# Products of zeros on an idle TensorE, GpSimd's sums in smaller pieces, and three placings moved, in an attention and expert kernel

## The chip, the cores and the metric

The kernel runs on one core of a Trainium2 chip. A core has five engines that run side by side, each through its own instructions in program order: TensorE (PE, matrix products and transposes), VectorE (DVE), ScalarE (ACT), GpSimd (POOL) and SyncE (SP), which here issues nearly all transfers. The metric is the device time of one execution in microseconds; the median over several runs is compared.

## The reference, cut to what matters

Attention over blocks, then a top-one mixture of experts, then a dense layer with a mish-like activation, each feeding the next:

```
k_sum = k.reshape(B, H, nb, 32, D).max(axis=3)        # 24 blocks of keys: maxima
v_sum = v.reshape(B, H, nb, 32, D).mean(axis=3)       # and of values: means
scores = [q k^T / 8 where |i - j| < 16, q k_sum^T / 8 + log 32]
a      = softmax(scores);  x = a [v, v_sum]           # B=2, H=8, S=768, D=64
logits = x w_gate + modality_bias[modality_id]        # 1536 tokens, 8 experts
out[e == argmax] = gate * (relu(x w1[e]) w2[e])       # 512 -> 1024 -> 512
h = out w_in;  y = (h * tanh(softplus(h))) w_out      # 512 -> 2048 -> 512
```

## The kernel before

The program has three stages that follow each other: attention with the gate (to about 130 us), the experts, the dense layer. The change touches the first alone. It is written by hand in the order in which each engine is to run: there is no scheduler, and an instruction waits only for what it reads or overwrites.

Attention goes through 24 groups (`groups`), each of 128 query positions of one batch and half of the heads (`hh`, four heads): six groups of batch 0 with half 0, six with half 1, then twelve of batch 1 with the halves in turn. The loop over `g` is a pipeline that runs two groups ahead: iteration g makes the scores of group g + 2, transposes the weights of group g (`transpose_a`, `store_aT`) and multiplies those of group g - 1 with the values (`values`, `store_xT`). Per group: `scores` (a bf16 product that lays the mask into PSUM, then q k in f32; both for four tiles), `top` (VectorE's row maximum `nm`), `exps` (ScalarE, with the row sum `sm`), `sums` (VectorE: a 128x4 addition and a reciprocal), `normalize` (`an`, on VectorE or GpSimd by the string `norm_by`). From group 10 on `gate_products` follows, which reads the tables `gm`; `choose` reads the table `bias_t`.

Queries and keys come in chunks of 256 positions (`c` = 0 to 2). A chunk (b, hh, c) is loaded by SyncE, packed by one engine (`pack`, tile `hp`), transposed on TensorE and copied from PSUM: `k_chunk` into `kt`, `q_chunk` in two halves of 64 partitions into one of four block-diagonal buffers `qb`. The table `prep` says in which iteration a chunk is taken up, who packs it and who copies: ("q", 1, 0, 0, "G", "VV") is packed by GpSimd, both halves copied by VectorE. Packs of `prep[g + 1]` stand at the start of iteration g, the transposes of `prep[g]` after its scores. "kw" entries make the block maxima (`k_maxima`), the overlapping windows of keys (`k_windows`, tile `kw`) and spread the maxima (`k_blocks`); they run one iteration after the one they are listed under.

The means of the values are made on GpSimd from a tile `vb` of 96 partitions (four heads of 24 blocks) x 32 positions x 64: `v_means` adds halves together, 16 + 16 positions (level 1, 1024 elements a partition), then 8 + 8, 4 + 4, 2 + 2, 1 + 1 and a scaling (level 2). Entries "m1" and "m2" of `prep` place the levels; there are four such sums, one for each batch and half, two of which run through both levels at once. The result is written to `vw` by four transfers (`store_means`), listed in `means_at`.

Ahead of the loop stand the loads of the first chunks, the first transposes, the scores of groups 0 and 1, and `small_loads` with `gate_tables` (the gate's identity columns, the modality's mask `mf`, its products `mt` and their sum `bias_t`, nine instructions on GpSimd). SyncE issues the loads in one order: those of the table `loads` for iteration g + 1 are issued at the start of iteration g, as far as buffers and the transfer queue let it run ahead.

## Time and profile before

| | before |
|---|---|
| median of three runs | 571.78 us (569.55 to 576.25) |
| profiled execution, device time | 573.32 us |
| its span, first to last instruction | 571.3 us |
| TensorE products busy | 533.4 us, 93% |
| VectorE busy | 390.7 us, 68% |
| ScalarE busy | 387.2 us, 68% |
| GpSimd busy | 95.5 us, 17% |

The page counts busy time over the whole span. Rows of the timeline give the start in us, the length in us, engine, line of the kernel, operation, tile written <- tiles read, shapes and a count of instructions merged into the row; in brackets the idle time of the engine ahead of it and what ended that. "PEclk" is the share of full speed that TensorE's clock was granted: 1.00 is 2.4 GHz, 0.5 is 1.2 GHz. The record of the clock begins at its first change; the first 23 us read 1.00 for that reason alone.

### The profile page before, as it was taken

How to read it: one execution, taken by the hardware profiler on the slowest of the kernel's cores; microseconds unless marked ns; L12 is line 12 of the kernel's file. 1: busy time of each engine (PE TensorE's matmuls, PEld its weight loads, DVE VectorE, ACT ScalarE, POOL GpSimd, SP SyncE). 2: the span in 40 equal slices, each digit the busy share in tenths (PEclk: the TensorE clock that was granted, in tenths of full speed). 3: DMA queues.
4: the chain of work that ended last, by engine and by line, in shares of the span. 5: the costliest groups of instructions: out<-in, count | busy, mean ns of one | idle time of the engine just before them, and what ended most of it. 6: DMA issues, size and time to landing. Idle time of an engine off the chain costs nothing.

```text
span 571.3 us, 9001 instructions
## 1 busy us (share of the span) xinstructions
PE 533.4 (93%) x3086; PEld 462.7 (81%) x3086; DVE 390.7 (68%) x905; ACT 387.2 (68%) x793; POOL 95.5 (17%) x138
## 2 busy tenths in 40 slices
PE   4868799978999999999999999999999999999995
PEld 3857798868979998899988888888888888888883
DVE  3686889877777767688879998645664466456442
ACT  4756867566554535465578999778877887887771
POOL 5485542240604100000000000004000002100003
PEclk9998899989999999999999999999999999999999
DMA  8999961265754967634332331001000000100001
GB/s 210 176 226 205 181 107 37 75 170 183 242 178 142 335 198 244 211 121 129 111 112 80 104 107 41 1 1 73 1 0 1 0 2 37 38 0 1 0 1 73
DMA packets 75888, 59.34 MB, mean 104 GB/s; under 512 B 28838, under 2 KB 66214, under 8 KB 75456
## 3 DMA queue, kind: packets, MB, share of 16 engines
q1 hardware_dynamic: 73200, 52.36, 34.3%
q0 software_dynamic: 2640, 6.38, 3.2%
q8 instruction: 25, 0.41, 0.3%
q14 instruction: 23, 0.19, 0.1%
HBM read 51.25 MB, written 6.29 MB: 101 GB/s over the span
## 4 chain that ended last, share of the span: by engine, by line
PE 51%; DVE 2%; ACT 2%; issue 1%; POOL 0%; POOLq 0%; DVEq 0%
PE ph L539 22%; PE o L1719 22%; PE ph L467 4%; PE o L485 3%; ACT L577 0%; DVE l L418 0%; DVE cin L520 0%; DVE xg L580 0%; POOL out_dram L1736 0%; DVE mol L491 0%; ACT cin L516 0%; ACT xg L571 0%; ACT xg L577 0%; POOLq L1811 0%; DVE cin L519 0%
## 5 line engine op out<-in xcount | busy, mean ns | idle before, releaser
L580 DVE TENSOR_TENSOR xg<-xg,ph 128x512 f32<-128x512 f32 x48 | 30.8, 684 | 94.5 <-ACT xg L577 94.5
L571 ACT ACTIVATE xg<-ph,cf 128x512 f32<-128x512 f32 x48 | 33.0, 688 | 38.7 <-PE ph L539 38.0
L1736 POOL DMA_INDIRECT out_dram<-ot,rows x9 | 10.8, 1204 | 245.6 <-DVE xh L561 87.2
L467 PE MATMUL ph<-xh,h 128*128 128x290 f32 x160 | 50.2, 313 | 0.3 <-issue 0.3
L467 PE MATMUL ph<-xl,h 128*128 128x290 f32 x160 | 47.6, 297 | 0.4 <-DVE xl L451 0.4
L467 PE MATMUL ph<-xh,l 128*128 128x290 f32 x160 | 47.6, 298 | 0.3 <-DVE l L418 0.3
L1195 ACT ACTIVATE a<-ps,nm 128x120 f32<-128x120 f32 x96 | 33.4, 362 | 18.6 <-DVE nm L1187 12.1
L1181 PE MATMUL ps<-kw,qb 128*128 128x120 f32 x192 | 41.1, 342 | 5.1 <-DVE qb L1124 3.1
L1181 PEld LDWEIGHTS ps<-kw,qb 128*128 128x128 f32 x192 | 34.8, 227 | 7.7 <-ACT xT L1249 2.2
L539 PE MATMUL ph<-moh,l 128*128 128x512 f32 x96 | 38.0, 396 | 0.0
L1719 PE MATMUL o<-h,gl 128*128 128x512 f32 x96 | 37.9, 395 | 0.0
L1719 PE MATMUL o<-h,gh 128*128 128x512 f32 x96 | 37.9, 395 | 0.0
L1719 PE MATMUL o<-l,gh 128*128 128x512 f32 x96 | 37.9, 395 | 0.0
L539 PE MATMUL ph<-mol,h 128*128 128x512 f32 x96 | 37.9, 395 | 0.0
L539 PE MATMUL ph<-moh,h 128*128 128x512 f32 x96 | 37.9, 394 | 0.0
L417 ACT CAST h<-cout 128x512 fp32r<-128x512 f32 x32 | 19.8, 620 | 20.9 <-PE o L485 15.0
L539 PE MATMUL ph<-moh,xh 128*128 128x512 f32 x96 | 31.9, 393 | 0.0
L539 PE MATMUL ph<-moh,xl 128*128 128x512 f32 x96 | 31.9, 393 | 0.0
L467 PEld LDWEIGHTS ph<-xh,h 128*128 128x128 f32 x160 | 30.4, 190 | 1.4 <-issue 1.0
L467 PEld LDWEIGHTS ph<-xl,h 128*128 128x128 f32 x160 | 30.4, 190 | 1.3 <-issue 0.7
L572 ACT ACTIVATE xg<-xg 128x512 f32<-128x512 f32 x48 | 30.4, 632 | 1.5
L577 ACT ACT_TABLE_LOAD x24 | 30.8, 1283 | 0.4
(333 smaller groups left out, 1605.4 us busy)
## 6 DMA issues: line engine op xcount, KB each, us to landing
r<-in_moe_w_dram SPq DMA_DIRECT2D x32, 256.0 KB
cr<-in_moe_w_in_dram SPq DMA_DIRECT2D x16, 512.0 KB
cr<-in_moe_w_out_dram SPq DMA_DIRECT2D x16, 512.0 KB
cout<-in_moe_w_dram SPq DMA_DIRECT2D x16, 256.0 KB
cin<-in_moe_w_dram SPq DMA_DIRECT2D x16, 256.0 KB
k<-in_k_dram SPq DMA_DIRECT2D x12, 256.0 KB
q<-in_q_dram SPq DMA_DIRECT2D x12, 256.0 KB
vb<-in_v_dram SPq DMA_DIRECT2D x4, 768.0 KB
```

The costliest lines, as they stand in the source:

```text
L417: A.copy(out=h, in_=r)
L467: T.matmul(ph[:, :W], a[:, kk, :], b[:, kk, :], start=n == 0, stop=n == 11)
L485: T.matmul(po[d][:, :W], a[:, d * 128:(d + 1) * 128], b, start=f == 0 and n == 0, stop=f == F // 128 - 1 and n == 2)
L539: ins.append(T.matmul(pt, a[:, kk, :], b[:, kk, c0:c0 + 512], start=n == 0, stop=n == 11))
L571: A.activation(out=t, in_=hps, func=AF.Sigmoid, bias=cf[:, C_B0:C_B0 + 1])
L572: A.activation(out=t, in_=t, func=AF.Arctan)
L577: A.activation(out=t, in_=t, func=AF.Sin, scale=2.0)
L580: V.tensor_tensor(out=t, in0=t, in1=ph.pop(u), op=ALU.mult)
L1181: T.matmul(o, qc[:, j, t % 4, :], kw[b, hh][:, j, t, :], start=False, stop=True)
L1195: A.activation(out=a[:, j], in_=ps[:, j, 0:KC], func=AF.Exp, bias=nm[:, j:j + 1], accum_out=sm[:, j:j + 1],)
L1719: T.matmul(acc[m], a[:, m * 128:(m + 1) * 128], b, start=f == 0 and n == 0, stop=f == NF2 - 1 and n == 2)
L1736: ins = G.indirect_dma_start(out=out[:, :], out_offset=bass.IndirectOffsetOnAxis(ap=at_rows, axis=0), in_=ot[:, :], in_offset=None,)
```

## The change

There are four edits, all in the attention stage.

1. `v_means` on GpSimd works in pieces of four positions, 256 elements a partition. The first level becomes four instructions, the second two, the third stays one (it had 256 elements).
2. In `prep`, the copies of the chunk of queries (0, 1, 0) go from ScalarE alone to ScalarE and VectorE, those of (1, 0, 0) from VectorE alone to ScalarE and VectorE, and (1, 1, 0) is taken up in iteration 10 and no longer in 9.
3. A tile of zeros, and `spin(n)`, which makes n products of it (bf16, 128x128 by 128x512) into a PSUM tile that nobody reads, under the tag of the tile `pv`. There are 31 such products, in seven places ahead of the loop.
4. `gate_tables` is called at the end of iteration 5 and no longer ahead of the loop. `small_loads`, and so the order of SyncE's transfers, stays.

```diff
-                    o = t[:, 0:n, :] if n > 1 else m.unsqueeze(1)
-                    G.tensor_tensor(out=o, in0=t[:, 0:n, :], in1=t[:, n:2 * n, :], op=ALU.add)
+                    for i in range(0, n, 4):
+                        k = min(n, i + 4)
+                        o = t[:, i:k, :] if n > 1 else m.unsqueeze(1)
+                        G.tensor_tensor(out=o, in0=t[:, i:k, :], in1=t[:, n + i:n + k, :], op=ALU.add)
                     n //= 2
@@
-            3: [("q", 0, 1, 0, "G", "AA"), ("k", 1, 0, 0, "G", "V"), ("m2", 0, 1)],
+            3: [("q", 0, 1, 0, "G", "AV"), ("k", 1, 0, 0, "G", "V"), ("m2", 0, 1)],
@@
-            9: [("kw", 1, 1, 1, "A"), ("kw", 1, 1, 2, "V"), ("k", 1, 1, 2, "G", "A"), ("q", 1, 0, 0, "G", "VV"), ("q", 1, 1, 0, "A", "VV")],
-            10: [("m2", 1, 1)],
+            9: [("kw", 1, 1, 1, "A"), ("kw", 1, 1, 2, "V"), ("k", 1, 1, 2, "G", "A"), ("q", 1, 0, 0, "G", "AV")],
+            10: [("q", 1, 1, 0, "A", "VV"), ("m2", 1, 1)],
@@
+        zeros = soon.tile([128, 512], BF16, tag="zeros", name="zeros", bufs=1)
+        V.memset(zeros, 0.0)
+        idle = ps_x.tile([128, 512], F32, tag="pv", name="idle")
+
+        def spin(n):
+            for _ in range(n):
+                T.matmul(idle, zeros[:, 0:128], zeros, start=True, stop=True)
@@
+        spin(8)
         for c in range(2):
             pack("k", 0, 0, c, "V")
             k_chunk(0, 0, c, "A", True)
+            spin(1 + c)
         pack("k", 0, 0, 2, "V")
         pack("q", 0, 0, 0, "V")
         k_chunk(0, 0, 2, "A", True)
+        spin(2)
         for c in range(3):
             first_maxima(c)
         k_windows(0, 0, 0, "A")
         q_chunk(0, 0, 0, "AV", True)
+        spin(6)
@@
         scores(0)
         scores(1)
+        spin(8)
         top(0)
         exps(0)
         pack("q", 0, 0, 1, "V")
         q_chunk(0, 0, 1, "VV", True)
+        spin(4)
@@
         mb_mi = small_loads()
-        gate_tables(*mb_mi)
-
@@
             if g in means_at:
                 store_means(*means_at[g])
+            if g == 5:
+                gate_tables(*mb_mi)
```

How the instructions stand then. TensorE, at the first transposes of keys (line 1064; `zeros` and `idle` are the new tiles). Before, right from the start:

```order
L1064 MATMUL pid<-cf,hp 128x128 x4
L1064 MATMUL px<-cf,hp 128x128 x4
L1064 MATMUL ps<-cf,hp 128x128 x8
L1180 LDWEIGHTS cb
L1180 MATMUL ps<-cb 128x120
```

Of the change, behind the first eight products of zeros:

```order
L1064 MATMUL pid<-cf,hp 128x128 x4
L1500 LDWEIGHTS zeros
L1500 MATMUL idle<-zeros 128x512
L1064 MATMUL px<-cf,hp 128x128 x4
L1500 LDWEIGHTS zeros
L1500 MATMUL idle<-zeros 128x512
```

Each product of zeros stands in TensorE's order between two transposes, so a transpose whose keys are there waits for it.

GpSimd, from the first sum (`vb`, line 1155 before and 1157 now) to the normalizations of groups 2 and 3. Before:

```order
L1155 TENSOR_TENSOR vb<-vb 96x1024
L1155 TENSOR_TENSOR vb<-vb 96x512
L1155 TENSOR_TENSOR vb<-vb 96x256
L1155 TENSOR_TENSOR vb<-vb 96x128
L1155 TENSOR_TENSOR vm<-vb 96x64
L1158 TENSOR_SCALAR vm<-vm 96x64
L1390 TENSOR_SCALAR gm<-cf 128x128 x4
L1394 TENSOR_SCALAR mf<-mi 128x12
```

Of the change, the stretch that now holds the gate's tables, from the packing of queries in iteration 5 to the sum of batch 1, half 0, and the normalization of group 8:

```order
L1037 TENSOR_SCALAR hp<-q 128x512
L1392 TENSOR_SCALAR gm<-cf 128x128 x4
L1396 TENSOR_SCALAR mf<-mi 128x12
L1397 TENSOR_TENSOR mt<-mf,mb 128x96
L1396 TENSOR_SCALAR mf<-mi 128x12
L1397 TENSOR_TENSOR mt<-mf,mb 128x96
L1401 TENSOR_TENSOR bias_t<-mt 128x96
L1157 TENSOR_TENSOR vb<-vb 96x256 x7
L1157 TENSOR_TENSOR vb<-vb 96x128
L1157 TENSOR_TENSOR vm<-vb 96x64
L1160 TENSOR_SCALAR vm<-vm 96x64
L1211 TENSOR_TENSOR an<-a,sm 128x480
```

The tables have moved behind iteration 5, and the sum of 1024, 512 and 256 elements has become seven instructions of 256.

VectorE, at the copies of the first queries of batch 1 (`qb_117` is chunk (1, 0, 0), `qb_118` chunk (1, 1, 0)). Before:

```order
L1203 TENSOR_SCALAR sm<-sm 128x4
L1204 RECIPROCAL sm<-sm 128x4
L1187 TENSOR_REDUCE nm<-ps 128x4
L1097 TENSOR_REDUCE ks<-kt 128x2x8 x2
L1124 TENSOR_SCALAR qb_117<-ps 64x2x8x32 x2
L1124 TENSOR_SCALAR qb_118<-ps 64x2x8x32 x2
```

Of the change, the same place and the iteration behind it:

```order
L1097 TENSOR_REDUCE ks<-kt 128x2x8 x2
L1124 TENSOR_SCALAR qb_117<-ps 64x2x8x32
L1205 TENSOR_SCALAR sm<-sm 128x4
L1206 RECIPROCAL sm<-sm 128x4
L1189 TENSOR_REDUCE nm<-ps 128x4
L1097 TENSOR_REDUCE ks<-kt 128x2x8 x2
L1103 COPY kw<-kt 128x2x5x96
L1108 COPY kw<-ks 128x24x24
L1124 TENSOR_SCALAR qb_118<-ps 64x2x8x32 x2
```

One copy of four stays in its place, one has gone to ScalarE, and two stand an iteration later, behind its windows.

## Rows read from the trace of the kernel before

**Rows 1.** Stretches of the span: length; busy time and instructions by engine; clock; DMA.

```profile
40.30:47.10 6.80, 6.15 (x30) 5.53 (x29) 4.16 (x8) 3.74 (x13) 4.04 (x7) 0.51 1.00 236
47.10:67.60 20.50, 15.86 (x137) 14.70 (x135) 17.59 (x28) 14.42 (x50) 12.83 (x14) 0.99 1.00 178
67.60:74.40 6.80, 5.90 (x29) 5.76 (x30) 5.73 (x12) 6.33 (x24) 2.43 (x3) 0.51 1.24 231
...
135.00:571.30 436.30, 424.91 (x2275) 362.75 (x2273) 287.46 (x606) 298.69 (x482) 35.16 (x52) 1.00 0.27 88
```

**Rows 2.** Timeline of TensorE, the four rows that waited longest in 24:80.

```profile
30.42 0.65 PE L1216 MATMUL pa<-cf,an 128*120 128x128 f32 x4 [1.78 <-POOL an L1209]
...
38.37 0.45 PE L1181 MATMUL ps<-kw,qb 128*128 128x120 f32 x2 [2.04 <-DVE kw L1108]
...
55.17 0.63 PE L1064 MATMUL px<-cf,hp 128*128 128x128 f32 x4 [2.33 <-DVE kt L1082]
...
68.50 0.28 PE L1180 MATMUL ps<-cb 67*128 67x120 bf16 x1 [3.04 <-DVE qb L1124]
```

**Rows 3.** Timeline of VectorE beside GpSimd's sums, and the query halves.

```profile
49.71 2.75 DVE L1209 TENSOR_TENSOR an<-a,sm 128x480 f32<-128x480 f32 x1
...
62.88 2.32 DVE L1203 TENSOR_SCALAR sm<-sm 128x4 f32<-128x4 f32 x1
...
67.06 2.81 DVE L1124 TENSOR_SCALAR qb<-ps 64x512 f32<-64x512 f32 x4
```

**Rows 4.** VectorE's groups by shape in 80:130: count | busy us, mean ns | idle.

```profile
L1203 DVE TENSOR_SCALAR sm<-sm 128x4 f32<-128x4 f32 x10 | 1.7, 168 | 3.0 <-ACT a L1195 3.0
...
L1209 DVE TENSOR_TENSOR an<-a,sm 128x480 f32<-128x480 f32 x1 | 0.7, 657 | 0.0
```

**Rows 5.** Timeline of GpSimd: waits for transfers, and what stands behind them.

```profile
27.50 0.26 POOL L1394 TENSOR_SCALAR mf<-mi 128x12 f32<-128x12 int32 x1 [7.81 <-DMA mi<-in_moe_modality_id_dram]
...
33.61 0.62 POOL L1037 TENSOR_SCALAR hp<-k 128x512 f32<-128x512 f32 x1 [1.20 <-DMA k<-in_k_dram]
...
49.58 5.39 POOL L1155 TENSOR_TENSOR vb<-vb 96x1024 f32<-96x1024 f32 x4 [3.37 <-DMA vb<-in_v_dram]
...
55.46 0.24 POOL L1158 TENSOR_SCALAR vm<-vm 96x64 f32<-96x64 f32 x1
56.94 0.99 POOL L1209 TENSOR_TENSOR an<-a,sm 128x480 f32<-128x480 f32 x1 [1.24 <-DVE sm L1204]
...
72.96 1.15 POOL L1037 TENSOR_SCALAR hp<-q 128x512 f32<-128x512 f32 x1 [1.46 <-DMA q<-in_q_dram]
...
77.97 0.62 POOL L1037 TENSOR_SCALAR hp<-q 128x512 f32<-128x512 f32 x1
```

**Rows 6.** Waits of SyncE's queue in 20:75: us in total, times, longest.

```profile
SPq L1042 <- ACT qb L1122: 2.6, 1, 2.6
```

**Rows 7.** GpSimd's sums by shape in 0:80, columns as in rows 4.

```profile
L1155 POOL TENSOR_TENSOR vb<-vb 96x1024 f32<-96x1024 f32 x4 | 9.6, 2403 | 8.9 <-DMA vb<-in_v_dram 8.9
...
L1155 POOL TENSOR_TENSOR vb<-vb 96x512 f32<-96x512 f32 x4 | 5.6, 1410 | 0.2
...
L1155 POOL TENSOR_TENSOR vb<-vb 96x256 f32<-96x256 f32 x4 | 3.3, 813 | 0.3
```

**Rows 8.** Timeline of TensorE: a pair of score products in group 0 and in group 9.

```profile
12.32 0.73 PE L1181 MATMUL ps<-kw,qb 128*128 128x120 f32 x2
...
52.08 0.43 PE L1181 MATMUL ps<-kw,qb 128*128 128x120 f32 x2
```

**Rows 9.** Timeline of TensorE: where the packs and group 8's normalization are used.

```profile
34.29 0.66 PE L1064 MATMUL px<-cf,hp 128*128 128x128 f32 x4 [0.58 <-POOL hp L1037]
...
60.02 0.60 PE L1216 MATMUL pa<-cf,an 128*120 128x128 f32 x4
...
79.68 0.60 PE L1064 MATMUL ps<-cf,hp 128*128 128x128 f32 x4
...
83.86 0.60 PE L1064 MATMUL ps<-cf,hp 128*128 128x128 f32 x4
```

## The prediction, made before the changed kernel ran

> **What bounds the kernel now.** I read the windows first. From 135 us on TensorE is busy for 424.91 of 436.30 us. The stretch from 47.1 to 67.6 us is looser, 15.86 of 20.50 us, and beside it lie two, 40.3 to 47.1 and 67.6 to 74.4 us, where the granted clock is 0.51, the 1.2 GHz level, and TensorE is busy for 6.15 and 5.90 us at half pace [rows 1]. Every edit acts before 80 us, so the question is how far the work at 80 us comes forward; what stands behind it is TensorE's own work and moves along as it is.
>
> Next TensorE's rows in order of time, those that waited longest between 24 and 80 us: 3.04 us at 68.50 for query halves that VectorE copies, 2.33 us at 55.17 for a key copy of VectorE, 2.04 us at 38.37 for VectorE's window copies, 1.78 us at 30.42 for a weight normalization on GpSimd [rows 2]. So VectorE is what TensorE waits for. VectorE's rows say why: the normalization `an` that takes 0.66 us later takes 2.75 us at 49.71, and a 128x4 addition that takes 0.17 us takes 2.32 us at 62.88 [rows 3, 4]. GpSimd's first and longest sum of v begins at 49.58 [rows 5], and such an instruction lasts 2.40 us [rows 7]: VectorE's instruction seems to stand until that sum has ended, then runs at its usual pace.
>
> The third reading decides the size. GpSimd, in program order, waits three times for a transfer: until 33.61 for keys, until 49.58 for the values of batch one, until 72.96 for queries [rows 5]. The SyncE queue that issues these loads waits little for compute in 20 to 75 us, its longest wait is 2.6 us [rows 6], and its order is unchanged. So these three landings stay where they are, and compute that comes forward will meet them.
>
> **Sums in pieces.** A half head group's sum is now seven instructions of 256 elements where it had one of 1024, one of 512 and one of 256; the tail of 128, 64 and the scaling stays. By rows 7 that is 7 x 0.813 - (2.403 + 1.410 + 0.813) = +1.07 us of GpSimd, four times, 4.3 us in all. In return a VectorE instruction that meets a sum should wait for one piece, at most 0.81 us, where it waited up to 2.40. The three waits on VectorE are 2.0 + 2.3 + 3.0 = 7.3 us; if each leaves 0.81 behind, 4.9 us go.
>
> **Clock.** Both stretches at 1.2 GHz begin around such waits, those that end at 38.37 and 68.50 [rows 1, 2]. If the waits go and the clock stays up, the 6.15 + 5.90 us of busy time shrink by about half, 6.0 us. Together 10.9 us that could be gained if nothing else held.
>
> **Query placings.** Four query halves stand in one row of VectorE, 2.81 us, in front of the scores that wait 3.0 us [rows 2, 3]. One goes to ScalarE and two go a group later: 3 x 0.70 = 2.1 us off this wait (it is part of the 3.0), 1.4 us of it back in front of the next group's scores. The half of group 3 that goes from ScalarE to VectorE adds 0.70 us there ahead of a key copy; I take it as hidden, since VectorE will by then have finished its window copies early and TensorE stands at the landing of 33.61 anyway. Uncovered it costs 0.7.
>
> **Gate tables.** Behind the first sum GpSimd sits until 27.50 for the small load `mi`, 7.81 us, and the normalizations of groups 2 and 3 are queued behind it; TensorE waits 1.8 us for the first of them [rows 2, 5]. Moved behind group 5, the tables (nine small instructions, the one shown 0.26 us; I take 0.33 for each, 3.0 us) lie ahead of the second landing, before which GpSimd is idle for 3.37 us [rows 5]. They cost nothing there; without that cover they cost 3.0 us, late at the next sum. Their first reader is the gate product of group 10.
>
> **Zero products.** 31 are added: 8 before the first keys, 1, 2, 2 and 6 between the first transposes and the scores, 8 and 4 behind the first scores. The first score pairs take 0.73 us where they later take 0.43 [rows 8]; with the clock up from the start eight pairs come 2.4 us earlier. No row shows a bf16 product of 512 columns. By rows 8 (two passes of 120 columns in 0.43 or 0.73 us) I bound it by 0.22 and 0.73 us; I take 0.22: TensorE would be busy without a gap from about 1 us on, where before it stood until the first pack, so I expect its clock to rise before the scores. The twelve behind the scores then cost 2.6 us, about what the scores give back. None of this is worth more than its effect at the first landing: TensorE's key transposes at 34.29 had waited only 0.58 us, for the pack that follows the landing [rows 5, 9]. So the 1.8 us of the tables and the early clock turn into a longer wait there, some 3 us. What they still buy is VectorE's window copies done before GpSimd's next sum begins.
>
> **The sum, held against the landings.** Floor: the values land at 49.5. The sums behind took until 55.70 [rows 5], with pieces 56.77; the normalization of group 8 queued behind them ends at 57.76 instead of 57.93. TensorE used it at 60.02 [rows 9], so at this place it can be at most 2.26 us earlier. From there to the query transposes at 79.68 the 3.0 us wait (less two remainders of 0.81) goes, 1.4 us, and with the clock up another 2.95. That makes 3.7 or 6.6 us. Ceiling: the queries land at 72.9, their pack ends at 74.11, and TensorE uses it at 79.68, slack 5.57; the pack behind the last sum ends at 78.59 and is used at 83.86, slack 5.27 [rows 5, 9]. With pieces that sum is 2 x 0.813 - 1.410 = 0.2 us longer and the pack before it up to 0.5 shorter. So no more than about 5.4 us. Between 3.7 and 5.4 I take 4.6 us. The profiled execution took 573.32 us, 2.0 more than its span of 571.3, and lies 1.5 above the median of 571.78; a saving in its rows is a saving in either: 571.8 - 4.6 = 567.2 us.
>
> **Rivals.**
> 1. *The clock falls again in the new waits.* At 34.29 TensorE would now wait some 3 us, and again some 2 to 3 us for group 8's normalization. For it: the drop of 40.3 followed a wait of 2.0 us, that of 67.6 fell into one of 3.0. Against: after 2.3 us at 55.17 the clock stayed up [rows 1, 2]. The Trainium skill (page "TensorE: Matmul & The Clock Gate", section "Why this matters for your kernels") advises against long idle gaps of TensorE between bursts, since the clock then returns to its lower level; by that rule the two longer waits undo what the products of zeros gave. The trace agrees for two of the three waits. Two such stretches cost what the two of before did: 2 to 3 us are left, 569.3 us.
> 2. *The landings move too.* If SyncE's queue is in truth held back by compute, the loads come earlier and most of the 10.9 us arrives: 562.5 us. For it: the one wait of 2.6 us in that queue [rows 6]. Against: its waits are few and short.
> 3. *The waits only change hands.* ScalarE or the pieces' remainders take TensorE's place: 571 us.
> 4. *Slower: the pieces interleave.* Nine GpSimd instructions where there were five can each stand behind a VectorE instruction of 0.66 us: 9 x 0.66 = 5.9 us, so the normalization of group 8 ends at 63.7 and TensorE's use moves from 60.02 to 63.7, +3.7 us; at the sum of 62 us once more 4 x 0.66 = 2.6. That gives about 578 us. It decides from the point where group 8's normalization ends later than 60.0. Against: VectorE will have done most of its copies before 49.5.
>
> **How the numbers follow.** The forecast 0.50 (565.5 to 569), rival 1 0.20, rival 2 0.13, rival 3 0.11, rival 4 0.06. One per cent, 5.7 us, is about what a measurement of this kernel can tell from no change (its three runs span 569.55 to 576.25). Below 566.1: rival 2 and a quarter of the forecast, 0.26. Above 577.5: part of rival 4, 0.04. The rest, 0.70, lies within. Range: rivals 1 and 3 and the forecast inside, 563.5 to 571.5 us.
>
> **What the new profile would show.** Right: VectorE's instructions beside the sums at most 0.81 us over their usual time; GpSimd's waits still ending at about 33.6, 49.6 and 73; group 8's normalization ending at 57 to 58; query transposes at 74 to 76 where they stood at 79.68; the clock at its upper level before the first scores. Wrong: landings that come earlier (rival 2), a granted clock of 0.5 behind 34 or 58 us (rival 1), sums that last over 9 us (rival 4), or zero products at the lower level in front of the scores.

## The result and the profile after the change

| | before | after |
|---|---|---|
| median, 20 executions each, beside one another | 571.84 us (567.22 to 576.25) | 573.91 us (570.33 to 577.25) |
| ratio after / before | | 1.0051 (95 % interval 1.0026 to 1.0076) |
| span of the profiled execution | 571.3 us | 573.8 us |
| TensorE products busy | 533.4 us | 539.0 us (31 products more) |
| VectorE, ScalarE, GpSimd busy | 390.7, 387.2, 95.5 us | 381.0, 387.1, 96.0 us |

The change makes the kernel slower by half a per cent, 2.9 us of 571.8. The forecast was 4.6 us faster, with a range that ends at 571.5: wrong in sign, and outside the range. A ratio leaves out executions that were disturbed, so it need not be the quotient of two medians.

The windows of the kernel after, with two stretches more than [rows 1] has (busy time and instructions of TensorE, its weight loads, VectorE, ScalarE, GpSimd; granted clock; DMA share; GB/s):

```profile
40.30:47.10 6.80, 5.56 (x49) 5.17 (x49) 2.83 (x8) 5.25 (x18) 5.64 (x15) 1.00 0.97 233
47.10:67.60 20.50, 14.53 (x100) 13.39 (x99) 10.99 (x24) 13.13 (x48) 12.88 (x21) 0.83 1.10 183
67.60:74.40 6.80, 6.16 (x42) 5.82 (x41) 5.14 (x12) 4.22 (x15) 3.35 (x5) 0.75 1.29 206
118.80:122.20 3.40, 2.74 (x24) 2.61 (x24) 2.92 (x12) 2.08 (x10) 2.21 (x3) 1.00 0.87 262
122.20:135.00 12.80, 9.20 (x42) 7.73 (x41) 5.74 (x17) 6.45 (x18) 0.99 (x1) 0.63 0.70 216
135.00:573.80 438.80, 427.67 (x2298) 366.00 (x2297) 289.65 (x615) 300.96 (x488) 35.45 (x52) 0.99 0.27 87
```

The last two stretches but one in the kernel before:

```profile
118.80:122.20 3.40, 3.40 (x18) 3.20 (x18) 3.34 (x21) 2.57 (x11) 2.38 (x3) 0.53 0.57 113
122.20:135.00 12.80, 10.22 (x81) 9.09 (x81) 9.35 (x29) 8.99 (x27) 1.97 (x2) 1.00 0.86 265
```

The two stretches at 1.2 GHz around 43 and 71 us are gone or halved, as forecast, but from 47.1 to 67.6 us the clock is now 0.83, and from 122.2 to 135 us, where it was 1.00, it is 0.63: there TensorE issued 42 products where it had issued 81. Of that, only the 3.4 us before it are given back, which were at 0.53 and are at 1.00. From 135 us on TensorE is as busy as before [rows 1].

TensorE's four longest waits in the first 140 us after the change, in its timeline:

```profile
32.84 0.66 PE L1064 MATMUL px<-cf,hp 128*128 128x128 f32 x4 [2.70 <-POOL hp L1037]
...
53.47 0.82 PE L1239 MATMUL pv<-aT,vw 120*128 120x128 f32 x4 [3.35 <-DMA vw<-vm]
...
67.13 0.48 PE L1183 MATMUL ps<-kw,qb 128*128 128x120 f32 x2 [2.23 <-DVE qb L1124]
...
126.02 0.32 PE L457 MATMUL ph<-cf,xg 34*128 34x34 f32 x1 [3.60 <-DMA xg<-xs,ids_early]
```

Two of the four are transfers that [rows 2, 5] did not lead me to: the block means of v (`store_means`, `vw<-vm`), which the values of group 6 read, and the last piece of the rows gathered for the first expert. In this execution group 8's scores start at 42.2 us where they started at 47.9, group 12's at 67.1 (68.6), group 23's at 117.1 (118.6), the first expert product at 136.6 (133.4). So 5.7 us are gained by group 8, 1.4 are left from group 14 on, and 4.7 are lost between group 23 and the first expert product.

### The profile page after: what moved, and what is told of

Read it like the earlier page. It is cut to its first block, busy times and chain, and to the rows that moved or that the text cites. A ratio compares the mean times of both kernels' runs of the same rounds, so it can differ in the third digit from the quotient of the medians.

```text
span 573.8 us, 9078 instructions
## 1 busy us (share of the span) xinstructions
PE 539.0 (94%) x3116; PEld 464.2 (81%) x3117; DVE 381.0 (66%) x906; ACT 387.1 (67%) x793; POOL 96.0 (17%) x154
## 4 chain that ended last, share of the span: by engine, by line
PE 51%; DVE 2%; ACT 2%; issue 1%; POOL 0%; POOLq 0%; DVEq 0%
PE ph L539 22%; PE o L1736 21%; PE ph L467 4%; PE o L485 3%; ACT L577 0%; DVE l L418 0%; DVE cin L520 0%; DVE xg L580 0%; POOL out_dram L1753 0%; DVE mol L491 0%; ACT cin L516 0%; ACT xg L571 0%; ACT xg L577 0%; POOLq L1828 0%; DVE cin L519 0%
## 5 line engine op out<-in xcount | busy, mean ns | idle before, releaser
L467 PE MATMUL ph<-xh,h 128*128 128x290 f32 x160 | 50.1, 313 | 0.0
L1183 PE MATMUL ps<-kw,qb 128*128 128x120 f32 x192 | 36.6, 315 | 4.3 <-DVE qb L1124 4.3
L1183 PEld LDWEIGHTS ps<-kw,qb 128*128 128x128 f32 x192 | 31.2, 204 | 6.7 <-DVE qb L1124 3.3
L1239 PE MATMUL pv<-aT,vw 120*128 120x128 f32 x192 | 30.4, 306 | 6.0 <-DMA vw<-vm 3.7
L1239 PEld LDWEIGHTS pv<-aT,vw 120*128 120x128 f32 x192 | 27.1, 216 | 7.5 <-issue 4.3
```

The costliest lines, as they stand in the source:

```text
L467: T.matmul(ph[:, :W], a[:, kk, :], b[:, kk, :], start=n == 0, stop=n == 11)
L1183: T.matmul(o, qc[:, j, t % 4, :], kw[b, hh][:, j, t, :], start=False, stop=True)
L1239: T.matmul(pv[:, 2 * j + n, :], w, aT[0:KC, 2 * j + n, :])
```

## Experiments

Every kernel ran 12 times beside 23 to 35 executions of the kernel before on the same chip. "Ratio" is to that kernel, with a 95 % interval; it is not the quotient of the medians (for b_half below that quotient is 1.0038, the ratio 1.0007), so differences of a few tenths of a per cent are read with their intervals. The starts of scores are those of one profiled execution.

### Each part alone

Four kernels: the kernel before with one part of the change each, as the diff shows it (sums in pieces; products of zeros; the gate's tables behind group five; query placings).

> The kernel before with GpSimd's sums in pieces of 256 alone. Theory H (hand-over): the change's loss comes from the stretch between 118 and 138 us, where the wait for the last gather piece and 10.2 us at the lower clock take back what was won; any of the four parts costs nothing by itself. The pieces alone then shorten VectorE's stalls of 2.3 to 2.8 us behind a whole sum to under 0.9 us, lengthen each sum on GpSimd by about 1.07 us, start group 12's scores 0 to 1 us before the 68.57 us of the kernel before, and end within 1 us of 571.8. Rival P (the pieces themselves): their 4.3 us more on GpSimd delay the normalizations and placings behind them; group 12 then starts later than 68.6 us and the time is 573 to 575.

> The kernel before with the products of zeros alone. Theory H: the granted clock is 1.0 from about 6 us on instead of from 23, group 3's scores start 2.5 to 3.5 us earlier than 23.71 us; what is left of it at group 12 is at most 1.4 us, because the landings behind 32 us do not move; the time is decided by the clock between 118 and 138 us: 571 if that stretch has at most 3.4 us at the lower clock, 573.5 to 574.5 if it has about 10. Rival Z (the products themselves cost): group 3's scores start no earlier than 23.7 us and everything behind them later, 573 to 575 without a longer stretch at the lower clock behind 118 us.

> The kernel before with the gate's tables moved behind group five alone. Theory H: the 7.81 us that GpSimd waited for the tables' small load at 27.5 us go, so the packing in front of the half-one keys starts at once when their landing (33.6 us) comes; group 8's scores start 0 to 4 us before the 47.91 us of the kernel before, group 12's at most 1.5 us before 68.57, and the time is 570.5 to 572.5. Rival: the tables behind group five stand in front of the block sums of batch one and delay the first normalization there (group 8's, which ended at about 56.9 us); group 12 starts later than 68.6 us and the time is 573 to 574.

> The kernel before with the query placings moved alone (one ScalarE half to VectorE in group 3, one VectorE half to ScalarE and one chunk a group later in groups 9 and 10). Theory H: TensorE's wait for the queries in front of group 12 (3.04 us at 68.5) becomes about 2.2 us, group 12 starts 0.5 to 1 us before 68.57 us, and the time is within 1 us of 571.8. Rival: the half that goes to VectorE in group 3 delays the scores of groups 4 to 7 by 0.5 to 1 us and the chunk in group 10 is late for its group; 572.5 to 573.5.

(In the third, the "half-one keys" are the first keys of batch one.)

| part alone | median | ratio | group 8 | group 12 | group 13 | group 23 | first expert product |
|---|---|---|---|---|---|---|---|
| pieces | 570.92 | 0.9997 (0.9967 to 1.0027) | 43.3 | 67.7 | 72.4 | 115.6 | 131.6 |
| zeros | 572.19 | 0.9992 (0.9963 to 1.0021) | 44.8 | 65.6 | 71.3 | 113.9 | 133.2 |
| tables | 571.91 | 1.0004 (0.9968 to 1.0040) | 45.2 | 68.9 | 73.6 | 116.8 | 135.5 |
| placings | 575.56 | 1.0076 (1.0043 to 1.0109) | 47.3 | 68.1 | 76.1 | 118.9 | 136.2 |

Three parts are worth nothing that can be measured, and the query placings alone cost 0.76 %, 4.3 us. That speaks for neither expectation in full: my theory H said that no part costs by itself. Its tie to the clock missed too: the profile with the zeros alone has 10.3 us at the lower clock (121.7 to 132.0) and took 572.5 us, not 573.5 to 574.5. Where the placings lose, their own profile shows: TensorE's timeline in front of groups 12 and 13,

```profile
68.09 0.78 PE L1181 MATMUL ps<-kw,qb 128*128 128x120 f32 x2 [4.67 <-DVE qb L1124]
...
76.08 0.48 PE L1181 MATMUL ps<-kw,qb 128*128 128x120 f32 x2 [1.27 <-DVE qb L1124]
```

ScalarE ahead of the first,

```profile
62.21 0.99 ACT L1103 COPY kw<-kt 128x960 f32<-128x960 f32 x1
64.93 0.67 ACT L1108 COPY kw<-ks 128x576 f32<-128x576 f32 x1 [1.73 <-DVE ks L1097]
65.51 0.67 ACT L1103 COPY kw<-kt 128x576 f32<-128x576 f32 x1
66.20 0.61 ACT L1082 COPY kt<-pid 128x512 f32<-128x512 f32 x1
66.70 0.61 ACT L1122 ACTIVATE qb<-ps 64x512 f32<-64x512 f32 x1
```

VectorE's own half for the first,

```profile
67.34 0.70 DVE L1124 TENSOR_SCALAR qb<-ps 64x512 f32<-64x512 f32 x1 [1.86 <-ACT qb L1122]
```

and VectorE ahead of the second:

```profile
71.37 1.27 DVE L1097 TENSOR_REDUCE ks<-kt 128x16 f32<-128x512 f32 x2
72.55 0.73 DVE L1103 COPY kw<-kt 128x960 f32<-128x960 f32 x1
73.20 1.52 DVE L1108 COPY kw<-ks 128x576 f32<-128x576 f32 x1
74.64 1.38 DVE L1124 TENSOR_SCALAR qb<-ps 64x512 f32<-64x512 f32 x2
```

The half that went to ScalarE stands behind three copies of key windows and one of keys there, the second of which waits 1.73 us for VectorE's maxima; VectorE's own half (L1124), which writes the same buffer, stands idle for 1.86 us until ScalarE's is done. So the two halves do not run side by side. The chunk that went one group later stands behind VectorE's maxima and copies for the windows, 3.3 us of work, and comes out at 76.02, when group 13 has waited 1.27 us for it.

### The wait for the gathered rows

The second loss, 118 to 136 us, was tried by filling that wait: 24 products of constants that nothing reads, in the kernel before (f_before), after (f_after) and with the placings alone (f_queries). `fill` is true in the first gathered window only. A fourth kernel is the changed one with the placings put back (n_queries).

```diff
             n = min(128, W - 128 * c)
+            if c == NPIECE - 1 and fill:
+                for _ in range(24):
+                    T.matmul(room[:, W:512], cb[:, 0:128], cb[:, 0:512 - W], start=True, stop=True)
             T.transpose(pt[:, c * 128:c * 128 + n], xg[c][0:n, d * 128:(d + 1) * 128], ident[0:n, 0:n])
```

> The kernel before with 24 products of constants (222 columns each, 2.2 us in all at full clock) placed on TensorE between the second and the third transpose of the first gathered window, where it waited 2.40 us at 126.6 us for the last gather piece; nothing reads what they write. Theory H (the clock behind this wait decides): the lower clock behind 118 us shrinks from 3.4 us to nothing and the first expert product follows group 23's scores by 12.5 to 13.5 us instead of 14.8; the time falls by 1 to 2.5 us against the kernel before, since in its other executions the lower clock there may be longer. Rival N (the clock there decides nothing): the same time as before, or up to 1 us more.

> The changed kernel with the same 24 products in the same place, where it waited 3.60 us at 126.0 us and then had 10.2 us at the lower clock. Theory H: no lower clock from 118 to 136 us, the first expert product follows group 23's scores by at most 15 us instead of 19.5, the time falls by 3.5 to 5 us to 569 to 570.5 and is within 1 us of the kernel before with the same products. Rival N: the same time as the changed kernel, 573 to 574, and 2 us over the kernel before with the same products.

> The kernel before with the query placings moved, and with the same 24 products in the same place. With the placings alone it took 0.76 % (4.3 us) more than before, although group 23's scores in its profile began only 0.29 us later; behind them came 6.8 us at the lower clock. Theory H: with the products the loss falls to that of group 23, 0 to 1 us against the kernel before with the products. Rival Q (the moved placings cost 3 to 4 us themselves, in executions that the profile does not show): it still takes 3 to 4 us more than the kernel before with the products.

> The changed kernel with the query placings put back: the pieces, the zeros and the gate's tables together. Rival Q (the placings are what made the change slower): 569 to 571.5, no slower than before. Theory H (the parts do not matter for themselves, the place in time at which the gather wait falls does): 571 to 574.5, anywhere in between, with group 23's scores at 113 to 117 us, and with the time following the length of the lower clock between 118 and 138 us (3.4 us: 570; 10.2 us: 573 to 574).

| kernel | median | ratio | without the products | group 13 | group 23 | from there to the first expert product |
|---|---|---|---|---|---|---|
| f_before | 570.47 | 0.9962 (0.9926 to 0.9999) | 1 | 71.7 | 114.6 | 14.9 |
| f_after | 573.46 | 1.0000 (0.9967 to 1.0032) | 1.0051 | 76.1 | 119.0 | 14.7 |
| f_queries | 573.55 | 1.0022 (0.9988 to 1.0056) | 1.0076 | 76.1 | 119.4 | 14.8 |
| n_queries | 572.22 | 0.9987 (0.9956 to 1.0018) | | 71.1 | 114.5 | 18.3 |

The windows of f_after:

```profile
118.80:122.20 3.40, 2.46 (x21) 2.14 (x21) 3.37 (x21) 2.56 (x11) 2.79 (x3) 1.00 0.52 101
122.20:136.00 13.80, 13.40 (x112) 12.13 (x111) 10.35 (x35) 8.98 (x27) 2.01 (x3) 1.00 0.79 249
```

The products do what they were made for: the clock stays up, and the way from group 23 to the first expert product takes 14.7 us where it took 19.5 (14.3 to 19.5, 17.2 on the mean, in eleven profiles of this study without them; 14.6 to 15.6, 15.0 on the mean, in the eight with them). They take 0.4 to 0.5 % off each of the three kernels (each difference known to about 0.4 %), about the 2.2 us between those means. But, as far as these intervals tell, they take as much off the kernel before as off the others, so the clock there does not tell the kernels apart, and theory H falls as the explanation of the loss. Its profile of before was one of the luckier executions in that stretch (14.8).

Rival Q stands: with the products the placings still cost 0.60 % (1.0022 against 0.9962), and the changed kernel without them is no slower than before. Three pairs that differ by the three placings alone give 0.76, 0.60 and 0.64 % (1.0051 against 0.9987), 3.4 to 4.3 us. A fourth pair does not: f_after (1.0000) differs from n_fill below (0.9995) by the placings alone too, and gives 0.05 %. Each of the four is known to 0.3 to 0.5 %, and their mean is 0.5 %, 2.9 us. Group 23 agrees with a loss: it starts at 117.1 to 119.4 us in the four profiles with the placings (118.6 on the mean), at 113.9 to 118.6 in the seven without them (115.6; n_fill is one of these).

### Which of the placings

u_half and u_late are the changed kernel with one placing put back; b_half, b_late and b_first the kernel before with one placing moved.

Moved half (b_half, u_late), from VectorE ("VV") to ScalarE and VectorE ("AV"):

```diff
-("q", 1, 0, 0, "G", "VV")
+("q", 1, 0, 0, "G", "AV")
```

Late chunk (b_late, u_half), from the list of group 9 to that of group 10:

```diff
-            10: [("m2", 1, 1)],
+            10: [("q", 1, 1, 0, "A", "VV"), ("m2", 1, 1)],
```

First (b_first, and in u_half and u_late too), a half for group 6:

```diff
-            3: [("q", 0, 1, 0, "G", "AA"), ("k", 1, 0, 0, "G", "V"), ("m2", 0, 1)],
+            3: [("q", 0, 1, 0, "G", "AV"), ("k", 1, 0, 0, "G", "V"), ("m2", 0, 1)],
```

> The changed kernel with one of the three moved placings put back: both halves of the queries in front of group 12 on VectorE again. Theory S (ScalarE's queue): where the first half is ScalarE's, it stands behind copies for which ScalarE waits on VectorE (1.73 us at 64.9 in the kernel with the placings alone), and group 12 waits 2.2 to 4.7 us for the queries; with all the other parts and both halves on VectorE it waited 0.60 us. So here the wait in front of group 12 falls below 1 us, and the time by at least half of the loss that the placings brought (0.64 %, 3.7 us): 570.5 to 572.3, a ratio of 0.997 to 1.002 to the kernel before. Theory L (the chunk that comes one group later is what costs): the wait in front of group 12 may shrink, but group 13 still waits about 1.2 us for its queries, and the time stays at 573 to 574.5.

> The changed kernel with another of the three placings put back: the chunk for group 13 in group 9 again, ahead of the copies of the keys' windows. Theory S: group 12 still waits 2 to 4.7 us for its queries, and the time is 573 to 575 (ratio 1.003 to 1.007). Theory L: group 13's wait (0.64 us in the changed kernel, 1.1 to 1.3 us in the two others with the placings) goes, group 13's scores follow group 12's by 4.7 us instead of 6.5 to 8.0, and the time is 570.5 to 572.5.

> The kernel before with one moved placing: the first half of the queries of group 12 (half-zero chunk of batch 1) from VectorE to ScalarE. Theory S+L (this half and the late chunk each cost about half of the 0.76 % of the three placings together): group 12 waits longer for its queries than the 3.04 us of the kernel before, or as long, because ScalarE comes to the half behind copies of windows that wait for VectorE; the time rises by 0.2 to 0.5 % (1 to 3 us). Theory S alone: 0.6 to 0.9 %. Theory L alone: 0 +- 0.2 %.

> The kernel before with one moved placing: the chunk of queries for group 13 one group later. Theory S+L: group 13's scores start 6.3 us or more behind group 12's (4.64 us where the chunk is a group earlier and the clock full), because VectorE comes to the chunk behind its copies of the windows; the time rises by 0.2 to 0.5 %. Theory L alone: 0.6 to 0.9 %. Theory S alone: 0 +- 0.2 %.

> The kernel before with one moved placing: the second half of the half-one queries of group 3 on VectorE instead of ScalarE. Theories S, L and S+L all leave it out: the same time within 0.2 %, groups 4 to 7 within 1 us of the kernel before. If it is this one that costs: 0.4 % or more, with group 6 to 8's scores later than 38.4 and 47.9 us.

| kernel | median | ratio | longest wait at group 12's scores | group 12 to group 13 |
|---|---|---|---|---|
| u_half: late and first moved | 573.44 | 1.0020 (0.9988 to 1.0052) | 1.07 | 6.3 |
| u_late: half and first moved | 573.77 | 1.0013 (0.9982 to 1.0043) | 1.85 | 5.2 |
| b_half: half alone | 575.58 | 1.0007 (0.9973 to 1.0040) | 1.93 | 4.6 |
| b_late: late alone | 574.71 | 1.0017 (0.9982 to 1.0053) | 2.34 | 7.5 |
| b_first: first alone | 572.51 | 0.9979 (0.9942 to 1.0015) | | |

The times don't part the placings: every interval holds 1. The two with one placing put back lie between the changed kernel and the one with all put back; the three with one moved lie about 1, and their sum of 0.03 % is not the 0.76 % of all three. At group 12 the waits came out otherwise than expected as well: 1.07 us for under 1, 1.85 for 2 to 4.7, 1.93 for 3.04 or more (the 2.34 of b_late was for a key copy of ScalarE, which ended 0.06 us behind the queries).

What the profiles do show is the place of the late chunk. Group 13 follows group 12 by 6.3 to 8.0 us in all six profiles of kernels that have it late. In those that have it early it does so by 4.3 to 4.7 us, and by 5.2 to 6.6 where the clock fell between the two groups (the kernel before, zeros, u_late, b_first, and n_best below). In u_half and b_late the clock was up there, and it is 6.3 and 7.5. b_late has that one edit alone; VectorE's queue and the product that waits:

```profile
69.91 1.27 DVE L1097 TENSOR_REDUCE ks<-kt 128x16 f32<-128x512 f32 x2
71.09 1.70 DVE L1103 COPY kw<-kt 128x960 f32<-128x960 f32 x1
72.71 0.97 DVE L1108 COPY kw<-ks 128x576 f32<-128x576 f32 x1
73.61 1.38 DVE L1124 TENSOR_SCALAR qb<-ps 64x512 f32<-64x512 f32 x2
```

```profile
75.05 0.48 PE L1181 MATMUL ps<-kw,qb 128*128 128x120 f32 x2 [2.96 <-DVE qb L1124]
```

For ScalarE's half the wait at group 12 shows it only beside the pieces: 1.85 and 2.23 us with it (u_late; after and f_after), 0.60 and 1.07 without (n_queries; u_half). With whole sums the wait is 1.9 to 4.7 with it and 0.6 to 3.0 without. VectorE's row shows it in every profile: in all six kernels with the half on ScalarE, VectorE idles 1.85 to 1.94 us for ScalarE's half and group 12's queries are ready 2.55 to 2.64 us after VectorE's maxima; in the fourteen without it there is no such idle time, and they are ready after 1.3 us. After the change, for one:

```profile
66.38 0.69 DVE L1124 TENSOR_SCALAR qb<-ps 64x512 f32<-64x512 f32 x1 [1.86 <-ACT qb L1122]
```

So each of the two delays its own group's scores. How much of the kernel's time each costs is not shown.

### What holds back the other three parts

The wait at 53.47 us is for the block means. SyncE's queue after the change, in order of issue (us, length, queue, line, transfer), and what the same queue becomes when the two loads of batch 1's values go behind the means (n_means_fill; the expectation calls them those of the values' other half):

```profile
40.87 0.94 SPq L1141 DMA_DIRECT2D vb<-in_v_dram  x2
41.91 0.39 SPq L1042 DMA_DIRECT2D k<-in_k_dram  x1
42.39 4.11 SPq L1165 DMA_DIRECT2D vw<-vm  x4
```

```profile
42.16 3.32 SPq L1168 DMA_DIRECT2D vw<-vm  x4
45.52 1.00 SPq L1144 DMA_DIRECT2D vb<-in_v_dram  x2
```

Each of the two loads is of 768 KB, each piece of the means of 72 KB. The means were issued at 42.4 to 46.5 us and used at 53.5. The Trainium skill (page "DMA: Bandwidth & Descriptors", section "Queues, rings and completion order") says that each DMA engine takes the descriptors of one ring in order; the traces agree, for with the order turned the means are issued at 42.2 us, nearly the same time, and TensorE, 3.4 us earlier, does not wait for them at all. The kernel before can meet this wait too: with the old order of loads it is 2.6 to 5.2 us in eleven profiles, f_before (3.50) and b_half (3.32) among them.

In `loads`, and in `prep` for GpSimd's sums of them:

```diff
-            5: [("vw", 0, 10), ("vb", 1, 0), ("vb", 1, 1), ("k", 1, 1, 1)],
+            5: [("vw", 0, 10), ("k", 1, 1, 1)],
+            6: [("vb", 1, 0), ("vb", 1, 1)],
...
-            5: [("m1", 1, 0), ("m2", 1, 0)],
-            6: [("k", 1, 0, 1, "A", "V"), ("q", 0, 1, 2, "G", "AV")],
+            6: [("k", 1, 0, 1, "A", "V"), ("q", 0, 1, 2, "G", "AV"), ("m1", 1, 0), ("m2", 1, 0)],
```

n_fill is n_queries with the 24 products; n_means_fill has this edit too; n_best moves the two loads further back, to loads 8, with the sums in groups 8 and 9, the means of batch 1's first half stored after group 9, and the normalizations of groups 10 and 11 on VectorE. b_means_fill is the kernel before with this edit and the 24 products, without any part of the change, and n_again is n_means_fill once more beside it.

> The changed kernel without its query placings, and with the 24 products of constants in the wait for the last gather piece. The kernel without the placings took 0.9987 of the kernel before (571.9 us by that), with 3.43 us of waiting at 123.5 us and 6.8 us at the lower clock behind it; the products took 0.38 to 0.54 % off three other kernels. If the two effects add, the ratio is 0.993 to 0.996 (568 to 570 us), with no lower clock from 118 to 136 us. If they do not, as much as the products win was already in it: 0.997 to 1.0.

> The same, and the loads of the values' other half (two of 768 KB) issued behind the four transfers of the block means instead of ahead of them, with GpSimd's sums of the first of them a group later. Theory W (the block means' landing holds back what the first 47 us win): TensorE's wait of 3.25 us at 54.5 us for the block means falls below 1 us, group 9 to 11's scores start 2 to 4 us earlier, group 23's at 111 to 113.5 us instead of 114.5, and the time is 566 to 569, 1 to 2.5 us less than without this edit. Rival G (the wait only moves): the queries and keys behind are no earlier, group 12 starts at 66 to 67 us as before with a longer wait in front of it or the sums are late for the means of the other half, and the time is the same as without this edit or up to 2 us more.

> The changed kernel without its query placings, with the 24 products in the gather wait, and the loads of the values' other half now also behind those of the keys and queries of groups 10 to 13; GpSimd's sums of them run three groups later and the normalizations of groups 10 and 11 are VectorE's. With the loads only behind the block means the ratio was 0.996 and TensorE waited 4.59 us at 60.3 us for keys that GpSimd packed behind the sums. Theory W (landings and what stands ahead of them on GpSimd limit this stretch): that wait goes, group 12's scores start at 60 to 63 us instead of 64.7, group 23's at 109 to 112 us instead of 113.1, the ratio is 0.990 to 0.995. Rival G: the sums that come later delay the next normalizations or the block means of the other half, group 23's scores start no earlier than 113 us, and the ratio is 0.995 or more.

> The kernel before with only the two edits that are not part of the change: the loads of the values' other half behind the block means, and the 24 products in the gather wait. Theory W (the landing of the block means held back what pieces, zeros and tables win): without them the scores of group 8 start at 44.5 to 48 us instead of 42.7, group 12's 1 to 3 us later than 64.7, group 23's at 114.5 to 116.5 instead of 113.1, and the time is 0.2 to 0.5 % above the kernel with all of them. Rival 0 (the three parts win nothing even then): the same time as that kernel within 0.15 %, and group 23's scores within 1 us of 113.1.

> The kernel with pieces, zeros and tables (no query placings), the loads behind the block means and the 24 products once more, beside the one without the three parts. It took 0.9961 of the kernel before (0.9936 to 0.9986). Theory W: again 0.993 to 0.998, and 0.2 to 0.5 % below the kernel without the three parts; group 23's scores at 112 to 114.5 us. Rival 0: the two are the same within 0.15 %.

| kernel | median | ratio | group 8 | group 10 | group 12 | group 23 |
|---|---|---|---|---|---|---|
| n_fill | 572.33 | 0.9995 (0.9966 to 1.0024) | 44.1 | 57.5 | 67.9 | 115.5 |
| n_means_fill | 570.16 | 0.9961 (0.9936 to 0.9986) | 42.7 | 51.2 | 64.7 | 113.1 |
| n_best | 572.06 | 0.9980 (0.9950 to 1.0011) | 42.2 | 52.3 | 61.8 | 113.6 |
| b_means_fill | 569.21 | 0.9946 (0.9925 to 0.9968) | 42.2 | 49.7 | 65.2 | 112.7 |
| n_again | 568.93 | 0.9943 (0.9916 to 0.9970) | 43.6 | 52.5 | 65.7 | 114.5 |

n_fill missed: the 24 products won nothing here. Its profile has no lower clock from 118 to 136 us, but a wait for a split weight further on, behind which the clock fell:

```profile
156.66 0.40 PE L470 MATMUL ph<-xh,h 128*128 128x290 f32 x1 [1.58 <-ACT h L417]
```

With the loads behind the means the values of group 6 start at 50.12 us in n_means_fill without a wait (first row below), group 10 six us earlier, and the kernel is faster than before, 0.54 to 0.57 % in the last pair. Theory W was right on the wait and wrong on the three parts: without them the time is the same (0.9946 and 0.9943), and group 23 starts no later. How much of the gain is the order of the loads is less clear: the products alone took 0.38 % off the kernel before (f_before), which leaves 0.16 % for it there; n_means_fill and n_again are 0.34 and 0.52 % below n_fill. Each of these differences is known to about 0.4 %, so only the last is clear of the noise. What both then wait for is the same, keys whose packing GpSimd does behind its sums of batch 1's values. TensorE in n_means_fill, then b_means_fill and n_again:

```profile
50.12 1.16 PE L1242 MATMUL pv<-aT,vw 120*128 120x128 f32 x8
...
60.27 0.78 PE L1067 MATMUL pid<-cf,hp 128*128 128x128 f32 x4 [4.59 <-POOL hp L1040]
```

```profile
58.91 1.11 PE L1067 MATMUL pid<-cf,hp 128*128 128x128 f32 x4 [4.70 <-POOL hp L1040]
```

```profile
61.26 0.75 PE L1067 MATMUL pid<-cf,hp 128*128 128x128 f32 x4 [4.29 <-POOL hp L1040]
```

and GpSimd in n_means_fill:

```profile
51.59 6.12 POOL L1160 TENSOR_TENSOR vb<-vb 96x256 f32<-96x256 f32 x8 [0.82 <-DMA vb<-in_v_dram]
...
59.59 0.62 POOL L1040 TENSOR_SCALAR hp<-k 128x512 f32<-128x512 f32 x1
```

n_best takes that wait away and starts group 12 at 61.8 us, but waits 2.38 us there for queries and 1.80 us at 74.96 for a query pack, and is back at 113.6 us by group 23. That pack itself stood 7.66 us for its transfer, not for the later sums:

```profile
74.28 0.62 POOL L1040 TENSOR_SCALAR hp<-q 128x512 f32<-128x512 f32 x1 [7.66 <-DMA q<-in_q_dram]
```

So rival G is right in that each wait removed is met again one landing later, though not by the way it named. The kernel that is fastest beside the kernel before is the one with the loads behind the block means and the 24 products, with the change's three parts or without.

## Why the prediction was wrong

**Query placings: the step that failed in sign.** "One goes to ScalarE and two go a group later: 2.1 us off this wait" costed the halves where they leave and not what stands ahead of them where they arrive. In the profile of the placings alone that is 2.9 us of copies and a wait of 1.73 us on ScalarE, and for the later chunk 3.3 us of VectorE's maxima and copies. The overlap was wrong as well: VectorE's half does not run beside ScalarE's but waits for it, 1.86 us after the change, and the queries are ready 1.3 us later, counted from VectorE's maxima, than with both halves on VectorE. The part that I took as a gain of 2.1 us costs 3.4 to 4.3 in three pairs of kernels and nothing clear of the noise in a fourth, 2.9 on the mean. (The half for group 6, which I took as hidden, is: b_first took 0.9979.) With the sums in pieces and the placings left alone, all four halves on VectorE, the wait of 3.0 us [rows 2] is 0.60 (VectorE, then TensorE, in n_queries):

```profile
64.89 2.81 DVE L1124 TENSOR_SCALAR qb<-ps 64x512 f32<-64x512 f32 x4
...
66.33 0.23 PE L1182 MATMUL ps<-cb 67*128 67x120 bf16 x1 [0.60 <-DVE qb L1124]
```

These are the same 2.81 us as in [rows 3], but 2.2 us earlier. The wait is 0.60 with whole sums too, in f_before and in the tables alone. So the 3.0 us were not owed to the number of halves.

**The base: "a saving in its rows is a saving in either".** This failed, and with it the gain that was forecast: 4.6 us, where the three parts without the placings gave 0.7 (0.13 %). f_before is the same program as the kernel before up to 122 us, and its execution has other waits: 2.06 us for VectorE's window copies as in [rows 2], but 0.60 instead of 3.04 at group 12, and 3.50 us for the block means instead of 2.33 for the key copy. TensorE in f_before:

```profile
54.59 0.91 PE L1240 MATMUL pv<-aT,vw 120*128 120x128 f32 x4 [3.50 <-DMA vw<-vm]
...
66.95 0.23 PE L1183 MATMUL ps<-cb 67*128 67x120 bf16 x1 [0.60 <-DVE qb L1127]
```

So of the 7.3 us that I summed, 4.8 are not in this execution. Group 8 starts at 47.9, 44.7, 45.8 and 45.4 us in the four profiles of this program (before, f_before, b_half, b_late: 45.9 on the mean), at 42.2, 43.6, 42.6 and 43.4 in the four of the changed one (after, f_after, u_half, u_late: 42.9). The gain at group 8 is 3.0 us and not 5.7; at group 10, behind the block means, it is 57.7 against 56.7, 1.0 us (b_late and u_late have one pack in another place there).

**The three landings.** They came 1.0 to 2.3 us earlier than the prediction put them, at 32.1, 47.3 and 72.0 us. For the second that is not the change's doing: with this order of loads it comes at 46.9 to 50.1 us in the kernels without the change or with one part of it, at 47.3 to 49.3 in the changed ones (after, f_after, u_half), which does not speak for rival 2:

```profile
32.12 0.67 POOL L1037 TENSOR_SCALAR hp<-k 128x512 f32<-128x512 f32 x1 [3.54 <-DMA k<-in_k_dram]
...
47.28 5.48 POOL L1157 TENSOR_TENSOR vb<-vb 96x256 f32<-96x256 f32 x8 [0.77 <-DMA vb<-in_v_dram]
...
53.24 0.24 POOL L1160 TENSOR_SCALAR vm<-vm 96x64 f32<-96x64 f32 x1
53.56 0.99 POOL L1211 TENSOR_TENSOR an<-a,sm 128x480 f32<-128x480 f32 x1
...
71.96 0.80 POOL L1037 TENSOR_SCALAR hp<-q 128x512 f32<-128x512 f32 x1 [2.63 <-DMA q<-in_q_dram]
```

(GpSimd after the change.) The method was right, the list short: it held the transfers that GpSimd waits for [rows 5], and in the profile of before no engine waited for the block means, since TensorE came to them at 57.3 us, late for its other waits. A bound that is just not met is not in a list of waits.

**Pieces, tables, zeros.** Their mechanisms were right. The pieces cost less than forecast: the first sum of batch 1 took 6.20 us to 53.48 where the whole one took 6.12 [rows 5], +0.08 and not +1.07: its eight additions took 0.69 us each on the mean, where [rows 7] gave 0.81 for those of 256 elements; that was a mean of three of 0.72 to 0.78 us and one of 1.02. What VectorE loses beside them is at most 0.56 us an instruction between 27 and 75 us, where it lost 2.1 [rows 3, 4]:

```profile
34.14 0.73 DVE L1205 TENSOR_SCALAR sm<-sm 128x4 f32<-128x4 f32 x1
...
73.61 0.54 DVE L1205 TENSOR_SCALAR sm<-sm 128x4 f32<-128x4 f32 x1
...
74.40 1.05 DVE L1211 TENSOR_TENSOR an<-a,sm 128x480 f32<-128x480 f32 x1
```

The tables went in ahead of 47 us for nothing, and the clock was up before the first scores (a score pair 0.45 us at 11.13, where [rows 8] has 0.73). Only the sum was wrong: taken alone each is worth 0 within 0.4 %, together -0.13 % (-0.44 to +0.18). The wait for the block means takes part of what they win; but with that wait gone they still win nothing (n_again beside b_means_fill), and TensorE then waits 4.3 to 4.7 us for GpSimd's key pack, with them or without. Rivals 1 and 3 name what happened to them: waits change hands, and the clock falls in the new ones (0.83 and 0.75 in the windows above, around waits of 3.35 and 2.23 us). The Trainium skill's advice against long idle gaps of TensorE (page "TensorE: Matmul & The Clock Gate", section "Why this matters for your kernels") holds here: with the wait at 126 us filled the clock stayed up in every profile with the 24 products but one, b_means_fill, where it is 0.96 from 118 to 136 us.

**"What stands behind 80 us moves along as it is".** Wrong by what a second hand-over does: the query transposes of 79.68 [rows 9] came 1.4 us earlier, at 78.26, and the first expert product 3.3 us later. f_before shows that this wait costs about 2 us in the kernel before as well (0.38 %, 0.01 to 0.74), and the profiled execution of before happened to show little of it.

**Rival 4, the slower one,** had another mechanism, pieces that interleave, and its test (group 8's normalization later than 60.0 us) came out at 54.6. The slower side came from the part that I had counted as a gain.

What stays open is how the loss divides between ScalarE's half and the later chunk, why three placings together cost what single ones did not show, and why the pair of f_after and n_fill shows no loss.

## What to carry to other kernels

Cost a moved instruction by what stands ahead of it in the queue that it enters, at the moment that it is wanted, and not by its own length where it leaves. Before summing waits of one profile, take a second execution of the same program: here waits of 2.3 and 3.0 us in one were gone or 0.60 in the next. List every transfer with its issue and its first use, not only those that something waits for; the next bound is the one with the least slack, and small transfers that are wanted soon belong ahead of large ones that are wanted late (here that took away a wait of some 3 us; what it is worth in time is within the noise in two pairs of three).

## What the runs showed of the hardware

- Products of constants in a wait of TensorE hold its clock: 24 of 222 columns took 2.44 us, the wait behind them was 0.17 us, and the clock was 1.00 from 118.8 to 136 us where it had been 0.63 from 122.2 to 135; in seven of the eight profiles with the products it stayed up there. TensorE in f_after:

```profile
124.31 2.44 PE L459 MATMUL ph<-cb 128*128 128x222 bf16 x24
126.93 0.25 PE L460 MATMUL ph<-cf,xg 34*128 34x34 f32 x1 [0.17 <-DVE oh L1288]
```

- On GpSimd a sum in eight additions (seven of 256 elements, one of 128) took 5.48 us, the four they replace (1024, 512, 256, 128) 5.39 [rows 5]: more instructions for the same elements cost next to nothing there.
- Executions of one program differ by more than the change: group 8 of the kernel before starts between 44.7 and 47.9 us in four profiles, and its 20 times span 9 us.
- The first 8 products of zeros took 3.59 us, 0.45 each, the later ones 0.24 to 0.30 (six in 1.46 us, two in 0.59), between the bounds of 0.22 and 0.73 that the prediction gave.
